# Turning the exponentials of the packed queries: from TensorE to VectorE and DMAs, with the value products a half step later

## The chip, the cores and the metric

The kernel runs on one core of a Trainium2 chip. The metric is the time of one execution on the device in microseconds (us). Its engines are TensorE (PE in the profile, with PEld for its weight loads), VectorE (DVE), ScalarE (ACT), GpSimd (POOL) and SyncE (SP), which here only issues DMAs.

## The reference

Two attentions after each other, then a Fourier mix over the sequence and the model dimension, a normalization and a feed-forward network. Batch 8, 8 heads, 576 tokens, 64 dimensions a head (model dimension 512), 32 packed queries a head, all in float32:

```python
p_packed = sm_attn(p, k, v)            # 32 packed queries look at 576 keys and values
out = sm_attn(q, p_packed, p_packed)   # 576 queries look at the 32 packed rows
# sm_attn(q, k, v): softmax(q @ k.T / sqrt(64)) @ v
x = out, heads side by side            # (8, 576, 512)
u = x + real(fft(fft(x, axis=1), axis=2))
un = (u - mean(u)) / sqrt(var(u) + 1e-6)
result = u + relu(un @ w_ch1) @ w_ch2  # 512 -> 2048 -> 512
```

## The kernel before

**Tiles.** The 8 x 576 rows of `u` go through the feed-forward network in nine tiles of 512 rows. In a tile (`ffn`) 16 pairs of products follow each other: `up(j)` (12 matmuls of 512 columns into the buffer `ph`, L857) and `down(j-1)` (12 matmuls into `acc`, L874). After `up(j)` ScalarE makes `hh` from `ph` and VectorE `hl` (L863, L864); `down(j)` uses both, one pair later. `ph` has one buffer only, so the next matmuls into it wait until `hl` has been made.

**Fronts.** The attention and the Fourier mix of batch b (`front(b)`, a generator) are made piece by piece between these products: `front(0)` ahead of all tiles, and `front(t + 1)` in tile t, up to batch 7. After `up(j)` comes half step 2j, after `down(j-1)` half step 2j+1. Half steps 0 and 2 finish the batch before; from half step 1 on each takes the next piece of the string `ORDER[min(b, 2)]`, in which `y` ends a piece. A piece in an even half step so stands between an up and a down product, one in an odd half step between a down and an up product.

**The pieces that matter.** Heads are worked on in two groups of four (g = 0, 1); 4 heads x 32 packed queries fill 128 partitions.

- `S` (`scores`): scores of the packed queries with the keys, their maxima, and on ScalarE the exponentials `e1` (128 x 576, L349).
- `X` (`turned_scores`): TensorE turns `e1` by matmuls with the identity, four 128 x 128 blocks and one of 64 columns for each group (L360, L363); ScalarE and VectorE copy them to `e1T` (L366, L367); VectorE takes the reciprocals of the sums.
- `p0 p1` (`packed`): the value products, for each group 5 chunks of tokens x 4 heads, `po += e1T.T @ vt` (L383). Four chunks have 128 rows and the last one 64. Each float32 matmul runs as two passes.
- `d0 d1`, `g0 g1`: the packed values turned, and their spectra (`pg`).
- `U` (`queries`): scores of the 576 queries with the packed values. The 512-wide parts and one narrow tail go to the shared banks, the other tail takes the buffer of `ph`:

```python
tails = [bank("s2Tt")] + ([psf.tile([P, 512], F32, tag="ph", name="s2Tt")] if len(gs) == 2 else [])
```

- `e0 e1`, `m0 a0 m1 a1`: second softmax, mostly on VectorE (L444, L445, L457 to L461, L498, L500).

**Order.** For TensorE, VectorE, ScalarE and GpSimd the order written is the order run (`manual_schedule`). SP's DMAs are put in order by the scheduler, those under `keep_in_program_order` as written. All loads go through SP's one queue. Keys, values and queries of a batch share two buffers (`ld`): the value loads `vt` (640 KB each) wait until `S` has read the keys, the query loads `qt` until `p0` and `p1` have read the values. A round trip through DRAM exists already: `send` writes a block of `u` (`far`, 256 KB) and reads it back in four parts (`back`).

Of the kernel before, what the change touches and what calls it, by code (L numbers as in the profile page):

```python
# [17 lines left out]
P = 128  # L18
S = 576
# [22 lines left out]
         "H1 v2 W10 P1",  # L42
         "K0 K1 Q0 Q1 y S V0 V1 y X y p0 p1 y d0 d1 y g0 y U y g1 y e0 y e1 y y m0 y a0 y m1 y a1 y f0 y r0 y h0 y f1 y r1 y "
         "h1 y y",
         "S y X y p0 p1 y d0 d1 y g0 y U y g1 y e0 y e1 y y m0 y a0 y m1 y a1 y f0 y r0 y h0 y f1 y r1 y "
         "h1 y y")


# [35 lines left out]
def tile_kernel(ctx, tc, kpT, qT, v, w1, w2, tabH, tabL, tabR, tabF, tabB, tabT, sel, ident_d, out):  # L84
# [182 lines left out]
    def load(src, shape, name, place=None, pinned=False):  # L267
        if isinstance(place, tuple):
            t = spot(*place, shape)
        elif place:  # L270
            t = work.tile(shape, F32, tag=place, name=name, bufs=2)
        else:
            t = ld.tile(shape, F32, tag="ld", name=name)
        sent = nc.sync.dma_start(t, src)
        if pinned:
            tc.keep_in_program_order(sent)
        return t
# [6 lines left out]
    def front(b):  # L284
# [16 lines left out]
            kps[g] = load(kpT[b, :, 2 * g:2 * g + 2, :], [P, 2, S + NPK], "kp")  # L301

        def load_values(g):
            vts[g] = load(v[b, :, g], [P, 5, 4 * D], "vt", (g, 4) if b == 0 else None, b == 1)

        def load_queries(g):
            qts[g] = load(qT[b, :, 2 * g:2 * g + 2, :], [P, 2, S], "qt", (g, 7) if b == 0 else (2, 0) if b == 1 and g == 0 else (2, 2 * S / DM) if b == 1 else None)
# [18 lines left out]
        def scores(*gs):  # L326
# [11 lines left out]
            for g in gs:  # L338
# [13 lines left out]
                in_place("x", g, exps)  # L352
                e1s[g], sums[g] = e1, sm2

        def turned_scores(*gs):
            tp = {}
            for g in gs:
                tp[g] = bank("e1tp")
                for c in range(4):
                    nc.tensor.transpose(tp[g][:, c * P:(c + 1) * P], e1s[g][:, c * P:(c + 1) * P], ident)  # L360
            tq = bank("e1tq")
            for g in gs:
                nc.tensor.transpose(tq[:D, g * P:(g + 1) * P], e1s[g][:, 4 * P:S], ident)  # L363
            for g in gs:
                e1T[g] = work.tile([P, 5, P], F32, tag="att", name="e1T", bufs=ATT)
                nc.scalar.copy(e1T[g][:, 0:4, :].rearrange("p c k -> p (c k)"), tp[g])  # L366
                nc.vector.tensor_copy(e1T[g][:D, 4, :], tq[:D, g * P:(g + 1) * P])  # L367
            for g in gs:
                ri, sm2 = small.tile([P, 1], F32, tag="ri", name="ri"), sums[g]
                nc.vector.tensor_scalar(ri, sm2[:, 0:1], sm2[:, 1:2], 1e-9, ALU.add, ALU.add)  # L370
                nc.vector.reciprocal(ri, ri)
                rinv[g] = ri

        def packed(g):

            if g not in vts:
                load_values(g)
            vt = vts[g]
            po = bank("po")
            for c in range(5):  # L380
                kk = P if c < 4 else D
                for h in range(4):
                    nc.tensor.matmul(  # L383
                        po[h * NPK:(h + 1) * NPK, :D], e1T[g][:kk, c, h * NPK:(h + 1) * NPK],
                        vt[:kk, c, h * D:(h + 1) * D], start=(c == 0), stop=(c == 4),
                        tile_position=(0, h * NPK))
            pp2 = work.tile([P, 2, D], F32, tag="pp2", name="pp2")
            nc.vector.tensor_scalar(pp2, po[:, :D].unsqueeze(1).to_broadcast([P, 2, D]), rinv[g], None, ALU.mult)
            pp2s[g] = pp2

            def spread():
                bd = work.tile([P, 4, D], F32, tag="tmp", name="bd", bufs=3)
                nc.gpsimd.tensor_tensor(bd, pp2[:, 0:1, :].to_broadcast([P, 4, D]),
                                        bmask.unsqueeze(2).to_broadcast([P, 4, D]), ALU.mult)

                def diagonals():
                    bdh[g] = work.tile([P, 4 * D], F32R, tag="bdh", name="bdh")
                    bdl[g] = work.tile([P, 4 * D], F32R, tag="bdl", name="bdl")
# [158 lines left out]
        def folded_parts(g):  # L557
# [10 lines left out]
            def low():  # L568
# [2 lines left out]

            in_place("H", g, low)

        parts = {"S": lambda _: scores(0, 1), "U": lambda _: queries(0, 1), "X": lambda _: turned_scores(0, 1),
                 "s": scores, "t": turned_scores, "p": packed, "d": packed_parts, "q": queries, "e": less_one, "m": less_mean, "g": values_spectrum, "a": weights, "f": folded, "r": folded_rest,
                 "h": folded_parts,
                 "T": load_tables, "B": lambda _: load_turn(), "K": load_keys, "V": load_values,
# [91 lines left out]
            ypx["p", 0] = value(xh, xl, slice(1, 256, 2))  # L669
            ypx["q", 0] = value(oh, ol, slice(1, 256, 2), psf.tile([P, 512], F32, tag="ph", name="px"))  # L670

        parts["P"], parts["X"] = first_products, lambda _: first_values() if b == 0 else turned_scores(0, 1)

        def idle(n, gate=None):
            w = gate if gate is not None else ubuf[:, NU - 1, 256:256 + P]
# [371 lines left out]
def _prepare(q, k, v, p, moe_w_ch1, moe_w_ch2):  # L1047
# [3 lines left out]
    def heads(x):  # L1051
        return x.transpose(0, 2, 1, 3).reshape(B, x.shape[2], DM)[:, :, col]

    def pairs(x):
# [3 lines left out]

    vv = np.zeros((B, 5 * P, DM), v.dtype)
    vv[:, :S] = heads(v)  # L1060
    arrays = {
        "kpT": np.concatenate([pairs(k), pairs(p)], 3), "qT": pairs(q[:, :, np.array(TOK), :]),
        "v": vv.reshape(B, 5, P, 2, 4 * D).transpose(0, 2, 3, 1, 4),
        "w1": moe_w_ch1[col].reshape(4, P, NJ, P).transpose(1, 2, 0, 3).reshape(P, NJ, DM),
        "w2": moe_w_ch2[:, col].reshape(NJ, P, DM).transpose(1, 0, 2),
    }
# [39 lines left out]
```

## Time and profile before

| | us |
|---|---|
| median of 3 runs (lowest to highest) | 983.49 (982.37 to 985.61) |
| profiled execution, its time | 983.41 |
| profiled execution, its span | 981.6 |
| TensorE busy (share of the span) | 958.2 (98%) |
| VectorE, ScalarE, GpSimd busy | 574.6, 458.0, 462.0 |

A busy time counts a matmul from its start to its modelled end, and matmuls overlap: 512-column matmuls show some 0.39 us each, but start 0.23 us apart. What a piece costs TensorE is therefore read from start to start in the timeline. A tile lasts about 105.5 us: the outputs of the first, second and third tile are issued from 165.61, 271.00 and 376.56 us on. The names in a row are `written<-read`, and a bracket at its end is the idle time ahead of it with what ended it.

### The profile page before, as it was taken

What the parts mean: (1) busy time and instruction counts of PE and PEld (TensorE: products, weight loads), DVE (VectorE), ACT (ScalarE), POOL (GpSimd) and SP (SyncE); (2) the same over time, 40 slices, a digit from 0 to 9 for tenths busy, and PEclk for the clock granted to TensorE, in tenths of its full rate; (3) what the DMA queues carried; (4) which work ended last, traced back from release to release, by engine and by line L of the source; (5) the groups of instructions that cost most, each with busy time, mean ns of one, the idle gap of its engine ahead of it and who ended that gap; (6) DMA issues with size and microseconds to landing.
All of it is one profiled execution on the core that took longest, in us unless ns stands there. A gap on an engine that the chain in (4) does not pass through costs nothing.

```text
span 981.6 us, 15190 instructions
## 1 busy us (share of the span) xinstructions
PE 958.2 (98%) x5682; PEld 782.5 (80%) x5682; DVE 574.6 (59%) x1184; ACT 458.0 (47%) x942; POOL 462.0 (47%) x397
## 2 busy tenths in 40 slices
PE   7899999999999999999999999999999999999998
PEld 4777787788877887788778887878777888887886
DVE  5988966487547855594658665784559451413111
ACT  5677655444444445444534545444443443334331
POOL 3146534454445534653455444543455354444542
PEclk9999999999999999999999999999999999999999
DMA  9565211300141012210330013110301010101001
GB/s 353 213 224 200 89 44 48 137 22 13 44 146 52 22 44 97 100 44 1 133 108 18 26 59 130 52 65 22 110 37 43 23 65 1 57 29 44 1 1 43
DMA packets 36968, 72.60 MB, mean 74 GB/s; under 512 B 4240, under 2 KB 18448, under 8 KB 36896
## 3 DMA queue, kind: packets, MB, share of 16 engines
q1 hardware_dynamic: 35856, 70.34, 20.7%
q0 software_dynamic: 1040, 1.31, 0.4%
q8 instruction: 44, 0.72, 0.3%
q14 instruction: 28, 0.23, 0.1%
HBM read 55.38 MB, written 16.25 MB: 73 GB/s over the span
## 4 chain that ended last, share of the span: by engine, by line
PE 83%; DVE 12%; ACT 2%; DMA 1%; issue 1%; POOL 0%; ACTq 0%; DVEq 0%; SPq 0%
PE ph L857 35%; PE acc L874 34%; DVE hl L864 1%; DVE s L498 1%; PE po L383 1%; DVE w2f L203 1%; PE px L282 1%; PE px L280 1%; PE px L281 1%; DMA wst<-w 1%; PE s L322 1%; PE e1tp L360 1%; PE py L280 1%; PE py L282 1%; PE py L281 1%
## 5 line engine op out<-in xcount | busy, mean ns | idle before, releaser
L110 POOL TENSOR_TENSOR wr_l<-w2f,wr_h 128x512 fp32r<-128x512 f32 x144 | 188.6, 1310 | 300.4 <-ACT wr_h L107 300.2
L110 POOL TENSOR_TENSOR wr_l<-w1f,wr_h 128x512 fp32r<-128x512 f32 x144 | 200.4, 1392 | 188.5 <-ACT wr_h L107 173.2
L864 DVE SCALAR_TENSOR_TENSOR hl<-ph,hh 128x512 fp32r<-128x512 f32 x144 | 98.7, 686 | 307.7 <-ACT hh L863 307.3
L857 PE MATMUL ph<-uh,wr_h 128*128 128x512 f32 (+1 forms) x580 | 228.7, 396 | 6.7 <-DVE hl L864 4.1
L874 PE MATMUL acc<-wr_h,hh 128*128 128x512 f32 x576 | 226.1, 392 | 0.0
L857 PE MATMUL ph<-ul,wr_h 128*128 128x512 f32 (+1 forms) x580 | 224.9, 389 | 0.5 <-DVE ul L110 0.5
L874 PE MATMUL acc<-wr_h,hl 128*128 128x512 f32 x576 | 224.9, 390 | 0.0
L874 PE MATMUL acc<-wr_l,hh 128*128 128x512 f32 x576 | 224.7, 390 | 0.0
L857 PE MATMUL ph<-uh,wr_l 128*128 128x512 f32 (+1 forms) x580 | 224.6, 389 | 0.0
L863 ACT ACTIVATE hh<-ph 128x512 fp32r<-128x512 f32 x144 | 86.2, 598 | 246.2 <-PE ph L857 232.5
L107 ACT CAST wr_h<-w1f 128x512 fp32r<-128x512 f32 x144 | 89.3, 620 | 175.1 <-PE acc L874 89.9
L857 PEld LDWEIGHTS ph<-uh,wr_h 128*128 128x128 f32 x580 | 108.5, 188 | 43.0 <-DVE hl L864 7.8
L857 PEld LDWEIGHTS ph<-uh,wr_l 128*128 128x128 f32 x580 | 108.5, 188 | 23.2
L874 PEld LDWEIGHTS acc<-wr_h,hl 128*128 128x128 f32 x576 | 108.1, 188 | 23.2
L857 PEld LDWEIGHTS ph<-ul,wr_h 128*128 128x128 f32 x580 | 108.6, 188 | 21.4 <-DVE ul L110 1.0
L874 PEld LDWEIGHTS acc<-wr_h,hh 128*128 128x128 f32 x576 | 108.1, 188 | 21.7
L874 PEld LDWEIGHTS acc<-wr_l,hh 128*128 128x128 f32 x576 | 108.2, 188 | 21.0
L107 ACT CAST wr_h<-w2f 128x512 fp32r<-128x512 f32 x144 | 88.6, 615 | 34.1 <-PE acc L874 26.9
L254 ACT ACTIVATE junk<-ubuf,stat 128x512 f32<-128x512 f32 x36 | 25.8, 718 | 3.3 <-DVE stat L249 3.3
L920 DVE SCALAR_TENSOR_TENSOR ubuf<-acc,stat,ubuf 128x512 f32<-128x512 f32 x36 | 24.5, 742 | 2.2 <-PE acc L874 2.2
L498 DVE TENSOR_TENSOR s<-s,z 128x576 f32<-128x576 f32 x16 | 24.7, 1541 | 0.5
L110 DVE TENSOR_TENSOR yl<-py,yh 128x258 fp32r<-128x258 f32 x32 | 13.2, 425 | 19.5 <-ACT yh L107 18.8
(229 smaller groups left out, 1229.5 us busy)
## 6 DMA issues: line engine op xcount, KB each, us to landing
kp<-kpT SPq DMA_DIRECT2D x16, 608.0 KB, 4.9
out<-ubuf SPq DMA_DIRECT2D x36, 256.0 KB, 2.1
vt<-v SPq DMA_DIRECT2D x14, 640.0 KB, 5.1
qt<-qT SPq DMA_DIRECT2D x12, 576.0 KB, 4.8
far<-unt SPq DMA_DIRECT2D x26, 256.0 KB, 2.0
back<-far SPq DMA_DIRECT2D x104, 64.0 KB, 2.0
w1f<-w SPq DMA_DIRECT2D x9, 512.0 KB, 7.2
w2f<-w SPq DMA_DIRECT2D x9, 512.0 KB, 6.6
```

What stands on the lines that cost most here:

```text
L107: copied = nc.scalar.copy(hi, src)
L110: (lo_eng or nc.vector).tensor_tensor(lo, src, hi.bitcast(F32), ALU.subtract)
L254: nc.scalar.activation(junk, u, AF.Square, bias=st[:, 1:2], scale=-sign, accum_out=st[:, 2:3])
L280: nc.tensor.matmul(o, lh, rh, start=first, stop=False)
L281: nc.tensor.matmul(o, lh, rl, start=False, stop=False)
L282: nc.tensor.matmul(o, ll, rh, start=False, stop=last)
L498: engw[g].tensor_tensor(s2s[g], s2s[g], broadcast(zs[g]), ALU.mult)
L857: nc.tensor.matmul(ph[:, t], l[:, c * P:(c + 1) * P], r[:, c, t], start=(k == 0), stop=(k == 11))
L863: nc.scalar.activation(hh[:, :T], ph[:, :T], AF.Relu)
L864: nc.vector.scalar_tensor_tensor(hl[:, :T], ph[:, :T], 0.0, hh[:, :T].bitcast(F32), ALU.max, ALU.subtract)
L874: nc.tensor.matmul(acc[i], l[:, w], r, start=(j == 0 and k == 0), stop=(j == NJ - 1 and k == 2))
L920: nc.vector.scalar_tensor_tensor(u, acc[i], stat_of[key][:, 2:3], u, ALU.mult, ALU.add)
```

## The change

For batches 2 to 7 the exponentials are no longer turned by TensorE. VectorE transposes `e1` in blocks of 32 x 32 (`e1b`), SP writes the result to DRAM (`fare`, 288 KB a group) and reads it back in four parts a group, so that `e1T` has tokens on its partitions, head by head (`scores_away`, piece `D`). `D` stands in the first piece, directly behind `S`; the order of SP's queue is fixed as first value load, the two writes, the eight reads, second value load. `X` keeps only the reciprocals. The value products come in half step 5 instead of 4, and everything up to `e1` a half step later; one empty half step ahead of `m0` is dropped, so `m0` and what follows keep their places.

The last two chunks of the value products have 96 rows in these batches. In batches 0 and 1, which keep the matmuls, the last chunk has 128 rows, with 64 tokens that the fourth chunk holds already set against zeros in the values, and the last turning matmul takes 128 columns. The host lays the values out to match.

```diff
-         "S y X y p0 p1 y d0 d1 y g0 y U y g1 y e0 y e1 y y m0 y a0 y m1 y a1 y f0 y r0 y h0 y f1 y r1 y "
+         "S V0 D V1 y X y y p0 p1 y d0 d1 y g0 y U y g1 y e0 y e1 y m0 y a0 y m1 y a1 y f0 y r0 y h0 y f1 y r1 y "
...
-            vts[g] = load(v[b, :, g], [P, 5, 4 * D], "vt", (g, 4) if b == 0 else None, b == 1)
+            vts[g] = load(v[b, :, g], [P, 5, 4 * D], "vt", (g, 4) if b == 0 else None, b > 0)
...
+        def chunk_rows(c):
+            return P if c < 3 or b < 2 else P - 32
+
+        def scores_away(*gs):
+            blocks = {}
+            for g in gs:
+                blocks[g] = work.tile([P, S], F32, tag="att", name="e1b", bufs=ATT)
+                nc.vector.transpose(blocks[g], e1s[g])
+            fars = {}
+            for g in gs:
+                fars[g] = dr.tile([P, S], F32, tag="fare", name="fare")
+                tc.keep_in_program_order(nc.sync.dma_start(fars[g], blocks[g]))
+            for g in gs:
+                e1T[g] = work.tile([P, 4, 5, NPK], F32, tag="att", name="e1T", bufs=ATT)
+                wide = e1T[g].rearrange("k h c p -> k h (c p)")
+                for r in range(4):
+                    n = NPK * (5 if r < 3 else 3)
+                    at = 5 * NPK * r
+                    back = nc.sync.dma_start(wide[r * 32:(r + 1) * 32, :, 0:n],
+                                             fars[g][:, at:at + n].rearrange("(h k) n -> k h n", h=4))
+                    tc.keep_in_program_order(back)
...
-                nc.tensor.transpose(tq[:D, g * P:(g + 1) * P], e1s[g][:, 4 * P:S], ident)
+                nc.tensor.transpose(tq[:, g * P:(g + 1) * P], e1s[g][:, S - P:S], ident)
...
-                kk = P if c < 4 else D
+                kk = chunk_rows(c)
...
-        parts["P"], parts["X"] = first_products, lambda _: first_values() if b == 0 else turned_scores(0, 1)
+        parts["P"], parts["X"] = first_products, lambda _: first_values() if b == 0 else turned_scores(0, 1) if b == 1 else score_sums(0, 1)
```

How the instructions stand. First TensorE at `U` of batch 3, in the third tile; before, it stands between a down product (L874) and an up product (L857):

```order
L874 MATMUL acc_3075<-wr_l,hh 128x512
L874 MATMUL acc_3075<-wr_h,hl 128x512
L322 MATMUL s2Tt<-qt,ppT 32x64 [waits DMAHW0_49,DVE_49]
L322 MATMUL s2Tt<-qt,ppT 32x64 [waits DMAHW1_49,DVE_49]
L322 MATMUL s2Tt<-qt,ppT 32x64 x6
L322 MATMUL s2T<-qt,ppT 32x512 [waits DVE_49] x2
L322 MATMUL s2T<-qt,ppT 32x512 x6
L857 MATMUL ph<-uh,wr_h 128x512 [waits DVE_49]
L857 MATMUL ph<-ul,wr_h 128x512
```

The same place after the change, where L885 is the up product and L902 the down product:

```order
L885 MATMUL ph<-ul,wr_h 128x512
L885 MATMUL ph<-uh,wr_l 128x512
L322 MATMUL s2Tt<-qt,ppT 32x64 [waits DMAHW4_49,DVE_49]
L322 MATMUL s2Tt<-qt,ppT 32x64 [waits DMAHW5_49,DVE_49]
L322 MATMUL s2Tt<-qt,ppT 32x64 x6
L322 MATMUL s2T<-qt,ppT 32x512 [waits PE_49] x2
L322 MATMUL s2T<-qt,ppT 32x512 x6
L902 MATMUL acc_3071<-wr_h,hh 128x512
L902 MATMUL acc_3071<-wr_l,hh 128x512 [waits Pool_49]
```

`U` has changed sides: it follows an up product now. Of its first two rows the second writes the tail that lies in the buffer of `ph`, so its wait on VectorE is one for the reader of the `ph` last written.

Next SP's queue, in the second tile; before, the two value loads, then the two query loads, then the keys of the next batch:

```order
L274 DMA vt<-v 128x1280 [waits PE_49]
L274 DMA vt<-v 128x1280 [waits DMAHW6_49,PE_49]
L274 DMA qt<-qT 128x1152 [waits DMAHW7_49,DMAHW5_49,PE_49]
L274 DMA qt<-qT 128x1152 [waits DMAHW6_49,DMAHW0_49,PE_49]
L274 DMA kp<-kpT 128x1216 [waits DMAHW7_49,DMAHW1_49,PE_49]
L274 DMA kp<-kpT 128x1216 [waits DMAHW2_49,DMAHW0_49,PE_49]
```

The same stretch after the change (DMAHW0 to 7 are the semaphores that landings raise):

```order
L274 DMA vt<-v 128x1280 [waits PE_49]
L368 DMA fare<-e1b 128x576 [waits DMAHW6_49,DVE_49]
L368 DMA fare<-e1b 128x576 [waits DMAHW7_49,DVE_49]
L375 DMA e1T<-fare 32x4x160 [waits DMAHW0_49,DMAHW6_49,Activation_49,Pool_49]
L375 DMA e1T<-fare 32x4x160 [waits DMAHW1_49]
L375 DMA e1T<-fare 32x4x160 [waits DMAHW2_49]
L375 DMA e1T<-fare 32x4x96 [waits DMAHW3_49]
L375 DMA e1T<-fare 32x4x160 [waits DMAHW4_49,DMAHW7_49,Activation_49,Pool_49]
L375 DMA e1T<-fare 32x4x160 [waits DMAHW5_49]
L375 DMA e1T<-fare 32x4x160
L375 DMA e1T<-fare 32x4x96
L274 DMA vt<-v 128x1280 [waits DMAHW0_49,PE_49]
```

The second value load has moved behind ten DMAs, of which the first reads wait for the writes to land and the writes for VectorE. The query loads follow it as before.

Last VectorE at the same time, before: behind the maxima of the scores it makes the `hl` of the second up product.

```order
L343 TENSOR_SCALAR nb<-mx_1997 128x1 [waits DVE_49]
L341 TENSOR_REDUCE mx_2006<-acc_1942 128x1
L341 TENSOR_REDUCE mx_2006<-s_1980 128x1 [waits PE_49]
L343 TENSOR_SCALAR nb<-mx_2006 128x1 [waits DVE_49]
L864 SCALAR_TENSOR_TENSOR hl<-ph,hh 128x512 [waits Activation_49]
L761 TENSOR_TENSOR xa<-px,spec_1971 64x512 [waits PE_49]
```

And after the change, where L892 makes `hl`:

```order
L343 TENSOR_SCALAR nb<-mx_1997 128x1 [waits DVE_49]
L341 TENSOR_REDUCE mx_2006<-acc_1942 128x1
L341 TENSOR_REDUCE mx_2006<-s_1980 128x1 [waits PE_49]
L343 TENSOR_SCALAR nb<-mx_2006 128x1 [waits DVE_49]
L364 STREAM_TRANSPOSE e1b<-e_2002 128x576 [waits Activation_49]
L364 STREAM_TRANSPOSE e1b<-e_2011 128x576 [waits Activation_49]
L892 SCALAR_TENSOR_TENSOR hl<-ph,hh 128x512 [waits Activation_49]
L789 TENSOR_TENSOR xa<-px,spec_1971 64x512 [waits PE_49]
```

Two transposes, each of which waits for ScalarE's exponentials, now stand ahead of that `hl`.

More of the change, by code (lines that the diff above doesn't have):

```diff
@@ L362, in turned_scores, with score_sums @@
             for g in gs:
-                nc.tensor.transpose(tq[:D, g * P:(g + 1) * P], e1s[g][:, 4 * P:S], ident)
+                nc.tensor.transpose(tq[:, g * P:(g + 1) * P], e1s[g][:, S - P:S], ident)
             for g in gs:
-                e1T[g] = work.tile([P, 5, P], F32, tag="att", name="e1T", bufs=ATT)
-                nc.scalar.copy(e1T[g][:, 0:4, :].rearrange("p c k -> p (c k)"), tp[g])
-                nc.vector.tensor_copy(e1T[g][:D, 4, :], tq[:D, g * P:(g + 1) * P])
+                t = work.tile([P, 5, P], F32, tag="att", name="e1T", bufs=ATT)
+                nc.scalar.copy(t[:, 0:4, :].rearrange("p c k -> p (c k)"), tp[g])
+                nc.vector.tensor_copy(t[:, 4, :], tq[:, g * P:(g + 1) * P])
+                e1T[g] = t.rearrange("k c (h p) -> k h c p", h=4)
+            score_sums(*gs)
+        def score_sums(*gs):
             for g in gs:
@@ L380, in packed @@
             for c in range(5):
-                kk = P if c < 4 else D
+                kk = chunk_rows(c)
                 for h in range(4):
                     nc.tensor.matmul(
-                        po[h * NPK:(h + 1) * NPK, :D], e1T[g][:kk, c, h * NPK:(h + 1) * NPK],
+                        po[h * NPK:(h + 1) * NPK, :D], e1T[g][:kk, h, c, :],
                         vt[:kk, c, h * D:(h + 1) * D], start=(c == 0), stop=(c == 4),
@@ L572, in folded_parts @@
             in_place("H", g, low)
-        parts = {"S": lambda _: scores(0, 1), "U": lambda _: queries(0, 1), "X": lambda _: turned_scores(0, 1),
+        parts = {"S": lambda _: scores(0, 1), "U": lambda _: queries(0, 1), "D": lambda _: scores_away(0, 1),
                  "s": scores, "t": turned_scores, "p": packed, "d": packed_parts, "q": queries, "e": less_one, "m": less_mean, "g": values_spectrum, "a": weights, "f": folded, "r": folded_rest,
@@ L1060, in _prepare @@
     vv[:, :S] = heads(v)
+    first = np.concatenate([vv[:2, :4 * P], vv[:2, -D:], vv[:2, 4 * P:S]], 1)
+    first = first.reshape(2, 5, P, 2, 4 * D).transpose(0, 2, 3, 1, 4)
+    later = vv[2:].reshape(B - 2, 4, 5, 32, 2, 4 * D).transpose(0, 1, 3, 4, 2, 5).reshape(B - 2, P, 2, 5, 4 * D)
     arrays = {
         "kpT": np.concatenate([pairs(k), pairs(p)], 3), "qT": pairs(q[:, :, np.array(TOK), :]),
-        "v": vv.reshape(B, 5, P, 2, 4 * D).transpose(0, 2, 3, 1, 4),
+        "v": np.concatenate([first, later]),
         "w1": moe_w_ch1[col].reshape(4, P, NJ, P).transpose(1, 2, 0, 3).reshape(P, NJ, DM),
```

## The prediction

> **What bounds the kernel now.** I read the page first (engine shares, chain), then the list of what TensorE waits for, and then the timeline of one tile, the third (270 to 376 us).
>
> ```profile
> span 981.6 us, 15190 instructions
> PE 958.2 (98%) x5682; PEld 782.5 (80%) x5682; DVE 574.6 (59%) x1184; ACT 458.0 (47%) x942; POOL 462.0 (47%) x397
> PE 83%; DVE 12%; ACT 2%; DMA 1%; issue 1%; POOL 0%; ACTq 0%; DVEq 0%; SPq 0%
> PE ph L857 <- DVE hl L864: 4.1, 3, 1.5
> ```
>
> TensorE is busy for 98% of the span and carries 83% of the chain; its largest wait, for `hl`, is 4.1 us in all. So inside a tile a microsecond taken from TensorE's row of work is a microsecond of the result, and so is one of new waiting; what the other engines do counts only where TensorE comes to wait for it. The profiled execution took 983.41 us, 1.8 around its span, and stands beside the median of 983.49; my sum is made against 983.41.
>
> **Removed: the turning matmuls (X).** In six tiles, those that prepare batches 2 to 7:
>
> ```profile
> 281.69 0.39 PE L874 MATMUL acc<-wr_h,hl 128*128 128x512 f32 x1
> 281.92 1.03 PE L360 MATMUL e1tp<-ident,e 128*128 128x128 f32 x8
> 282.79 0.38 PE L363 MATMUL e1tq<-ident,e 128*64 128x128 f32 x2
> 282.93 0.48 PE L857 MATMUL ph<-uh,wr_h 128*128 128x512 f32 x1
> 283.24 0.40 PE L857 MATMUL ph<-ul,wr_h 128*128 128x512 f32 x1
> 283.48 0.40 PE L857 MATMUL ph<-uh,wr_l 128*128 128x512 f32 x1
> ...
> 285.87 1.73 PE L383 MATMUL po<-vt,e1T 128*32 128x64 f32 x80
> 287.53 0.50 PE L874 MATMUL acc<-wr_h,hh 128*128 128x512 f32 x1
> ```
>
> A 512-wide matmul follows the one before by 0.23 (281.69 to 281.92). With X gone the up product starts at 281.92 instead of 282.93, 1.01 us earlier, and its first step is 0.23 instead of 0.31 (the step out of the 64-column form): **1.10 us a tile**. The copies of the turned rows on ScalarE and VectorE go too; TensorE waits for neither here, so they count as nothing.
>
> **One tile size in the value products.** Windows cut narrowly into L383 show the passes of four:
>
> ```profile
> 285.87 0.65 PE L383 MATMUL po<-vt,e1T 128*32 128x64 f32 x32
> 286.29 0.42 PE L383 MATMUL po<-vt,e1T 128*32 128x64 f32 x7
> 286.46 0.26 PE L383 MATMUL po<-vt,e1T 64*32 64x64 f32 x4
> 286.54 0.42 PE L383 MATMUL po<-vt,e1T 64*32 64x64 f32 x7
> 286.70 0.26 PE L383 MATMUL po<-vt,e1T 128*32 128x64 f32 x4
> ...
> 273.31 0.40 PE L857 MATMUL ph<-uh,wr_l 128*128 128x512 f32 x1
> 273.54 0.41 PE L602 MATMUL pz<-yr,tbr 101*128 101x258 f32 x2
> ```
>
> Eight passes of 128 rows start between 285.87 and 286.29, 0.06 apart. The step into the 64-row form is 0.17 (286.29 to 286.46), the one after it 0.08, the step back 0.16 (286.54 to 286.70): some 0.13 too much for each of three changes inside the two products, **0.40 us a tile**. The last chunks now hold 96 rows. L602, with 101 rows, follows a 128-row matmul after the usual 0.23, so a count between 64 and 128 costs no change; I take 96 like 101.
>
> The two batches that keep the matmul way gain too: the one prepared in the first tile 0.40 and the 0.08 of the 64-column step, 0.5 us; the first batch, where TensorE waits for other engines around these matmuls, between nothing and two changes (0.26), taken as 0.1. Together 0.6 us.
>
> **Moved: everything from the value products to `e` by a half step.** This is where I see the price. The score products U write one of their tails into the only buffer of `ph`, which the up product also uses. Before, U stands behind a down product, and the `ph` that it needs was read out during that product. Now U stands directly behind an up product, and has to wait until that product's `hh` and `hl` have been made.
>
> ```profile
> 296.39 0.39 PE L874 MATMUL acc<-wr_h,hl 128*128 128x512 f32 x1
> 296.70 0.34 PE L322 MATMUL s2Tt<-qt,ppT 64*32 64x64 f32 x16
> ...
> 300.46 0.40 PE L857 MATMUL ph<-uh,wr_l 128*128 128x512 f32 x1
> 300.95 0.60 ACT L863 ACTIVATE hh<-ph 128x512 fp32r<-128x512 f32 x1 [3.22 <-PE ph L857]
> 301.58 0.69 DVE L864 SCALAR_TENSOR_TENSOR hl<-ph,hh 128x512 fp32r<-128x512 f32 x1 [2.23 <-ACT hh L863]
> ```
>
> U starts 0.31 after the matmul before it. Here the last matmul of the up product starts at 300.46, so U could start at 300.77; `hl` ends at 302.27, and with a hop of 0.03 (as from `hh` to `hl`) the second matmul of U starts at 302.30. TensorE executes in order, so the whole queue behind it (the rest of U, the next down product) waits: **1.53 us a tile lost**. This wait hangs only on rows that the change doesn't touch, so its bounds are narrow: 1.4 and 1.7. Nothing covers it, and no stall of TensorE goes away in exchange (U had none).
>
> **Added: transposes on VectorE, two writes and eight reads on SP's queue, the second value load behind them.** All of this has to be done before the value products, which stand a half step later.
>
> ```profile
> 277.65 0.20 ACT L349 ACTIVATION_READ_ACCUMULATOR e<-s,nb 128x1 f32 x1
> 278.60 0.21 ACT L349 ACTIVATION_READ_ACCUMULATOR e<-s,nb 128x1 f32 x1
> 279.33 0.69 DVE L864 SCALAR_TENSOR_TENSOR hl<-ph,hh 128x512 fp32r<-128x512 f32 x1 [1.68 <-ACT hh L863]
> 317.71 0.78 DVE L500 STREAM_TRANSPOSE a<-s 128x576 f32<-128x576 f32 x1
> ...
> 219.47 0.33 SPq L786 DMA_DIRECT2D far<-unt  x1
> 221.53 1.75 SPq L791 DMA_DIRECT2D back<-far  x4
> 257.79 3.71 SPq L791 DMA_DIRECT2D back<-far  x8
> 275.73 1.39 SPq L274 DMA_DIRECT2D vt<-v  x2
> back<-far SPq DMA_DIRECT2D x104, 64.0 KB, 2.0
> DMA to landing us min/median/max: 3.9/3.9/3.9
> DMA to landing us min/median/max: 4.7/4.7/4.7
> ```
>
> The transposes (0.78 each, the size of L500) start when the exponentials end, 277.85 and 278.81, and end at 278.65 and 279.6; they fill VectorE's 1.68 of idleness and push `hl` from 279.33 to about 279.6. Its `ph` is wanted at 281.92, so that is free. The first write is issued at 278.70. From the issue of `far` (256 KB) to the first read behind it pass 2.06; a load of 640 KB takes 3.9 to land, so 32 KB more are worth some 0.15, and a write of 288 KB 2.2. So the reads start at 280.9, eight take 3.71 as for `back`, and the second value load is issued at 284.6; before, it stood right behind the first one of 275.73. The two landing rows are those of this tile's first value load (3.9) and first query load (4.7, 576 KB), each ahead of its partner in the queue: 288.5 to 289.3, and I take 288.6, since the 3.9 is for the same 640 KB. TensorE, without X, would start the first value products at 287.5 (one up and one down product after 281.92) and the second, ten passes of 0.06 later, at 288.1. So it waits **0.5 us a tile** for values; the turned exponentials themselves (last read issued by 284.5, landing 2.0 later as `back` does) are in time. Behind the value load in SP's queue stand the query loads; they need the buffers of the value products anyway, so they are issued at 288.1 and some 289, land by 294 even with the 4.7, and U comes at about 300. Ends: nothing, if the reads issue or the load lands 0.5 faster, and 1.3, with the 4.7.
>
> The Trainium skill, page "VectorE: DVE Perf Modes", section "The three transpose paths", speaks against such a path: it sends a 128x128 transpose to TensorE where PSUM will do, and calls a plain DMA copy with a strided pattern 19 times slower than the hardware's DMA transpose. The round trip of this kernel, with 512-byte runs, doesn't show that price, and the new reads have runs of 640 and 384 bytes.
>
> **Later in the tile.** `e0` and `e1` now both stand between two `hl`.
>
> ```profile
> 620.66 1.57 DVE L445 TENSOR_TENSOR s<-s,m 128x576 f32<-128x576 f32 x1
> 623.80 0.74 DVE L444 TENSOR_REDUCE m<-s 128x18 f32<-128x576 f32 x1
> 624.58 1.08 DVE L445 TENSOR_TENSOR s<-s,m 128x576 f32<-128x576 f32 x1
> 628.57 0.69 DVE L864 SCALAR_TENSOR_TENSOR hl<-ph,hh 128x512 fp32r<-128x512 f32 x1 [2.91 <-ACT hh L863]
> ```
>
> They take 0.74+1.57+0.74+1.08, with gaps 4.2 us, in the 4.8 from 623.80 to 628.57: room of 0.6, or none if both subtractions take 1.57. I count nothing, and up to 0.3 us a tile at the other end.
>
> **Sum.** A tile: -1.10 -0.40 +1.53 +0.50 = +0.53; six tiles +3.2; the two other batches -0.6: +2.6, so 983.41 becomes 986.0, 0.26% more, just inside what a measurement of this kernel can tell from no change (about 0.3%, from 980.5 to 986.4).
>
> **Rivals.** (1) The values come in time, the 0.5 is nothing: 983.0. For it: 0.5 is the end of a chain of ten steps, each good to 0.1. (2) Slower: the second value load decides. If it lands like the query load, or the ten DMAs issue more slowly, TensorE waits 1.3 a tile: 6 x 0.8 more, 990.8. It makes the kernel measurably slower from 0.6 us a tile on. For it: of the two rows one shows 4.7. Against: the row of its own size shows 3.9. (3) Faster: U doesn't wait, since `ph` is free after all, and only the values cost: 986.0 - 9.2 = 976.8. Against it: the order shows U's second matmul behind the up product with a wait on VectorE, whose count in the built program is the one that this up product's `hl` raises. (4) 96 rows count as a tile size of their own: 2.4 more, 988.4. Against: the 101-row matmuls. (5) VectorE falls behind at `e1`: up to 1.8 more, 987.8. (6) The turning path is slow as such, a read taking 19 times the 2 us of `back`: e1T would come near 319, some 31 us late in each tile, +190 us. The skill's sentence above would say so; the rows of `back` say the opposite, and the runs here aren't single elements.
>
> **Chances.** Forecast (values 0.25 to 0.8 late; 984.5 to 987.8) 0.47; (1) 0.19; (2) 0.16; (3) 0.08; (4) 0.05; (5) 0.04; (6) 0.01. Faster by over 0.3%: (3), 0.08. Within: (1) and some 0.27 of the forecast, whose threshold lies at 0.57 us of waiting, 0.46. Slower: the rest, 0.46. The range from 982.0 (rival 1 with U's wait at 1.4) to 990.5 leaves out (3), (6) and the end of (2), about 0.15; the forecast's own range is 984.5 to 987.8.
>
> **What would show it.** In the profile after: L360 and L363 only in the first two batches, and up products that follow down products 0.23 later near 281.9; passes of the value products 0.06 apart without a long step; a TensorE wait of 1.5 us at U, put down to `hl`, in six tiles; one of about half a microsecond at the second value products, put down to the value load; `hl` before 280.4 in the third tile; no wait for `e1T`. I am wrong if U starts 0.31 behind the up product, if the second value load is issued before the reads, or if a new wait for VectorE shows late in the tiles.

## The result and the profile after

| | before | after |
|---|---|---|
| median of 6 runs each, us (lowest to highest) | 983.86 (982.37 to 985.61) | 989.73 (987.76 to 990.58) |
| ratio after to before, 95% interval | | 1.0061 [1.0049, 1.0074] |
| profiled execution, time / span | 983.41 / 981.6 | 989.80 / 988.0 |

The changed kernel is slower by 0.6%. The head of its page (span, busy times, chain) and the top of the list of what TensorE waits for (total, times, longest):

```profile
span 988.0 us, 15216 instructions
PE 951.6 (96%) x5622; PEld 776.0 (79%) x5622; DVE 581.3 (59%) x1184; ACT 452.2 (46%) x930; POOL 465.9 (47%) x397
PE 76%; DVE 12%; DMA 5%; ACT 3%; issue 1%; SPq 1%; POOL 0%; ACTq 0%; DVEq 0%
...
PE s2Tt L322 <- DVE hl L892: 7.5, 6, 1.2
PE po L411 <- DMA vt<-v: 5.0, 6, 1.4
```

TensorE has 60 matmuls and 6.6 us of work less, and the span is 6.4 longer. Two new waits, six times each, stand at the top: `U` for `hl`, and the value products for the value load. DMAs now carry 5% of the chain. No wait of the six tiles is put down to the reads of `e1T`. The third tile in the timeline (it starts at 273.44 instead of 270.81), first TensorE and VectorE:

```profile
280.51 0.78 DVE L364 STREAM_TRANSPOSE e1b<-e 128x576 f32<-128x576 f32 x1 [0.22 <-ACT e L349]
281.48 0.78 DVE L364 STREAM_TRANSPOSE e1b<-e 128x576 f32<-128x576 f32 x1 [0.19 <-ACT e L349]
282.18 0.65 DVE L892 SCALAR_TENSOR_TENSOR hl<-ph,hh 128x512 fp32r<-128x512 f32 x1
...
284.32 0.39 PE L902 MATMUL acc<-wr_h,hl 128*128 128x512 f32 x1
284.54 0.39 PE L885 MATMUL ph<-uh,wr_h 128*128 128x512 f32 x1
284.77 0.39 PE L885 MATMUL ph<-ul,wr_h 128*128 128x512 f32 x1
...
290.08 0.77 PE L411 MATMUL po<-vt,e1T 128*32 128x64 f32 x40
291.43 0.77 PE L411 MATMUL po<-vt,e1T 128*32 128x64 f32 x40 [0.59 <-DMA vt<-v]
...
301.31 0.30 PE L322 MATMUL s2Tt<-qt,ppT 64*32 64x64 f32 x2
302.11 0.69 DVE L892 SCALAR_TENSOR_TENSOR hl<-ph,hh 128x512 fp32r<-128x512 f32 x1 [1.11 <-ACT hh L891]
302.85 0.28 PE L322 MATMUL s2Tt<-qt,ppT 64*32 64x64 f32 x7 [1.25 <-DVE hl L892]
```

Where `X` stood, the up product (284.54) follows the down product at 0.22. The value products are two closed blocks of 40 passes without a long step inside, but apart: four heads run beside each other, so a block is ten steps of 0.06, the second could have started at 290.68 (290.08 and ten steps) and started at 291.43, 0.75 later. `U` begins at 301.31 and stands until `hl` has ended: 302.85, 1.54 later.

SP's queue in the same tile, and the landing of its first and of its second value load:

```profile
278.36 0.34 SPq L274 DMA_DIRECT2D vt<-v  x1
281.32 1.28 SPq L368 DMA_DIRECT2D fare<-e1b  x2
283.50 3.65 SPq L375 DMA_DIRECT2D e1T<-fare  x8
287.24 0.38 SPq L274 DMA_DIRECT2D vt<-v  x1
...
DMA to landing us min/median/max: 4.0/4.0/4.0
DMA to landing us min/median/max: 3.9/3.9/3.9
```

Counted from the first value load, the writes are issued at +2.96, the reads at +5.14, the second value load at +8.88; it lands at +12.8.

**The balance by tile.** From the first up product of a tile to the next one's, in us, tiles 1 to 8 (the fronts of batches 2 to 7 are made in tiles 2 to 7):

| tile | 1 | 2 | 3 | 4 | 5 | 6 | 7 | 8 |
|---|---|---|---|---|---|---|---|---|
| before | 115.40 | 105.55 | 105.56 | 105.07 | 105.07 | 106.94 | 106.84 | 88.79 |
| after | 115.52 | 106.84 | 106.32 | 106.87 | 106.15 | 106.82 | 107.57 | 88.79 |

The six tiles lose 5.5 us together. Ahead of the first tile another 1.2 are lost, and 0.5 come back behind the last.

### The profile page after: what moved, and what is told of

Same layout as the page of the kernel before. It is cut to its first block, busy times and chain, and to the rows that moved or that the text cites. A ratio compares the mean times of both kernels' runs of the same rounds, so it can differ in the third digit from the quotient of the medians.

```text
span 988.0 us, 15216 instructions
## 1 busy us (share of the span) xinstructions
PE 951.6 (96%) x5622; PEld 776.0 (79%) x5622; DVE 581.3 (59%) x1184; ACT 452.2 (46%) x930; POOL 465.9 (47%) x397
## 3 DMA queue, kind: packets, MB, share of 16 engines
q0 software_dynamic: 1040, 1.31, 0.4%
## 4 chain that ended last, share of the span: by engine, by line
PE 76%; DVE 12%; DMA 5%; ACT 3%; issue 1%; SPq 1%; POOL 0%; ACTq 0%; DVEq 0%
PE ph L885 33%; PE acc L902 32%; DMA vt<-v 2%; DVE hl L892 2%; DVE s L526 1%; SPq L375 1%; DMA w1f<-w 1%; DVE w2f L203 1%; PE px L282 1%; PE px L280 1%; PE px L281 1%; DMA wst<-w 1%; ACT hh L891 1%; DMA fare<-e1b 1%; PE py L280 1%
## 5 line engine op out<-in xcount | busy, mean ns | idle before, releaser
L110 POOL TENSOR_TENSOR wr_l<-w1f,wr_h 128x512 fp32r<-128x512 f32 x144 | 202.9, 1409 | 178.6 <-ACT wr_h L107 163.8
L892 DVE SCALAR_TENSOR_TENSOR hl<-ph,hh 128x512 fp32r<-128x512 f32 x144 | 98.6, 685 | 294.1 <-ACT hh L891 293.8
L885 PE MATMUL ph<-uh,wr_h 128*128 128x512 f32 (+1 forms) x580 | 228.0, 395 | 5.6 <-DVE hl L892 2.9
L902 PE MATMUL acc<-wr_h,hh 128*128 128x512 f32 x576 | 226.5, 393 | 0.0
L885 PE MATMUL ph<-ul,wr_h 128*128 128x512 f32 (+1 forms) x580 | 224.8, 389 | 0.5 <-DVE ul L110 0.5
L902 PE MATMUL acc<-wr_h,hl 128*128 128x512 f32 x576 | 224.9, 390 | 0.0
L902 PE MATMUL acc<-wr_l,hh 128*128 128x512 f32 x576 | 224.7, 390 | 0.0
L885 PE MATMUL ph<-uh,wr_l 128*128 128x512 f32 (+1 forms) x580 | 224.5, 389 | 0.0
L885 PEld LDWEIGHTS ph<-uh,wr_h 128*128 128x128 f32 x580 | 108.5, 188 | 38.2 <-DVE hl L892 7.8
L902 PEld LDWEIGHTS acc<-wr_h,hh 128*128 128x128 f32 x576 | 108.2, 188 | 26.5 <-issue 5.0
L885 PEld LDWEIGHTS ph<-uh,wr_l 128*128 128x128 f32 x580 | 108.5, 188 | 23.0
L902 PEld LDWEIGHTS acc<-wr_h,hl 128*128 128x128 f32 x576 | 108.2, 188 | 23.1
L885 PEld LDWEIGHTS ph<-ul,wr_h 128*128 128x128 f32 x580 | 108.6, 188 | 21.3 <-DVE ul L110 1.0
L902 PEld LDWEIGHTS acc<-wr_l,hh 128*128 128x128 f32 x576 | 108.2, 188 | 21.1
L508 DVE TENSOR_TENSOR turned<-pg,turn 128x516 f32<-128x516 f32 x32 | 20.7, 688 | 12.6 <-PE pg L503 12.2
```

What stands on the lines that cost most here:

```text
L110: (lo_eng or nc.vector).tensor_tensor(lo, src, hi.bitcast(F32), ALU.subtract)
L508: nc.vector.tensor_tensor(x, pg[:, :N2].unsqueeze(1).to_broadcast([P, 2, N2]), w, ALU.mult)
L885: nc.tensor.matmul(ph[:, t], l[:, c * P:(c + 1) * P], r[:, c, t], start=(k == 0), stop=(k == 11))
L892: nc.vector.scalar_tensor_tensor(hl[:, :T], ph[:, :T], 0.0, hh[:, :T].bitcast(F32), ALU.max, ALU.subtract)
L902: nc.tensor.matmul(acc[i], l[:, w], r, start=(j == 0 and k == 0), stop=(j == NJ - 1 and k == 2))
```

## The experiments

All were timed in five rounds against the kernel before on the same chip; its medians there were 983.66 (30 runs) for the first four, 983.5 (11) for the next four, 982.53 (11) for the last. A "gap" is from one matmul's start to the next one's.

**1. Query scores behind a down product.** `U` and `g0` change places, so that `U` stands where its buffer is free:

```diff
-  "S V0 D V1 y X y y p0 p1 y d0 d1 y g0 y U y g1 y ..."
+  "S V0 D V1 y X y y p0 p1 y d0 d1 y U y g0 y g1 y ..."
```

> The changed kernel with one swap: U in half step 7 (behind a down product) and g0 in half step 8; nothing else differs. Theory (U's second tail waits for the buffer of ph, 1.46 us in each of six tiles in the changed kernel's trace): the TensorE wait of U for hl is gone, U starts 0.3 us behind the down product, and the time falls by 6 x 1.46 = 8.8 us, from 989.7 to 981, which is 0.997 of the time before; the wait for the second value load stays at about 1 us a tile. Rival (the lost time is given back as a wait elsewhere, VectorE being late from the moved half step on): the wait at U goes, but waits of TensorE for VectorE grow later in the tiles and the time stays above 986, ratio over 1.002.

Measured: 982.01 us (979.12 to 985.22), ratio 0.9982 [0.9969, 0.9996]. Its waits of TensorE:

```profile
PE po L411 <- DMA vt<-v: 5.1, 6, 1.2
...
PE ph L885 <- DVE hl L892: 4.1, 3, 1.5
```

The wait of `U` is gone from the list, the wait for the values stands as it was. From its first matmul to the product behind it `U` takes 1.26 us on the mean of the six tiles instead of 2.67, together 8.5 less, and the six tiles are 7.7 shorter. 1.2 are paid elsewhere: the gap ahead of an up product late in the sixth tile, 0.75 in the changed kernel, is 1.91 again, as it was before (last section).

**2. Both value loads first.** `V1` ahead of `D`, all else as in the changed kernel:

```diff
-  "S V0 D V1 y X ..."
+  "S V0 V1 D y X ..."
```

> The changed kernel with the second value load moved ahead of the two writes and eight reads in SP's queue (V0 V1 D); nothing else differs. Theory (the second value load is issued 8.9 us behind the first and its landing ends TensorE's wait at the second value products, 5.9 us over six tiles): it is issued 0.4 us behind the first, the wait for vt goes, and the reads of e1T land by some 0.4 us before the products need them; the time falls by 5 to 6 us to about 984, ratio 1.000 to 1.002. The wait at U stays at 1.46 a tile. Rival (the reads then come late, since the writes queue behind 640 KB more on the DMA engines): TensorE waits for e1T in place of vt, by 0.5 us or more at each of the value products, and the time stays at 987 to 990.

Measured: 986.54 us (985.09 to 989.59), ratio 1.0036 [1.0023, 1.0048]. A wait of TensorE, the third tile in SP's queue, and the writes in the list of DMAs (KB each, median us from issue to landing):

```profile
PE po L411 <- DMA e1T<-fare: 2.3, 3, 1.2
...
275.97 1.61 SPq L274 DMA_DIRECT2D vt<-v  x2
278.93 1.29 SPq L368 DMA_DIRECT2D fare<-e1b  x2
284.37 3.64 SPq L375 DMA_DIRECT2D e1T<-fare  x8
...
fare<-e1b SPq DMA_DIRECT2D x12, 288.0 KB, 3.9
```

The wait for the values is gone from the list, and half of it comes back as a wait for `e1T` (from start to start 3.1 us in the six tiles, where 6.0 were lost to the values). The writes land 3.9 us after issue on the median instead of 2.1; in the third tile it is 5.4, and the reads start at +8.4 there instead of +5.1. So both were half right: in two tiles nothing waits, as the theory had it, and in four the products wait 0.3 to 1.4 us, two of them over the 0.5 of the rival.

**3. Both edits together.**

```diff
-  "S V0 D V1 y X y y p0 p1 y d0 d1 y g0 y U y g1 y ..."
+  "S V0 V1 D y X y y p0 p1 y d0 d1 y U y g0 y g1 y ..."
```

> Both moves at once: the second value load ahead of the writes and reads, and U in half step 7 with g0 behind it. Theory (the two waits are all that eats the gain): no wait of TensorE over 0.2 us in the six tiles up to e1; the gain of 1.1 us (turning matmuls) and 0.4 us (tile size) a tile is seen whole, 6 x 1.5 and 0.6 in the other batches: 974 to 976, ratio 0.990 to 0.993 of the time before. Rival (the gain is lost to VectorE late in the tiles, where e0 and e1 now follow each other directly): waits of TensorE for hl late in the tiles grow, and the time stays at 979 or more, ratio over 0.995.

Measured: 979.72 us (975.61 to 984.24), ratio 0.9957 [0.9939, 0.9974]: less gain than the theory had, and the time of the rival, but not by its mechanism. TensorE's wait for `hl` late in the tiles is 4.1 us, no more than the 4.1 of the kernel before. What is left at the value products is the wait of experiment 2:

```profile
PE po L411 <- DMA e1T<-fare: 3.2, 4, 1.0
```

Against the changed kernel the six tiles gain 8.9 us, where the two waits were worth 15. From start to start the value products still wait 3.8, `U` takes 1.8 more than before the change (in two tiles it also waits for a query load, 0.5 each), and the sixth tile's gap is 1.91 again.

**4. One tile size alone.** The kernel before, with 128 rows in all chunks of the value products, in all batches, and 128 columns in the last turning matmul; matmuls still turn the exponentials, and the host lays the values out to match:

```diff
-                nc.tensor.transpose(tq[:D, g * P:(g + 1) * P], e1s[g][:, 4 * P:S], ident)
+                nc.tensor.transpose(tq[:, g * P:(g + 1) * P], e1s[g][:, S - P:S], ident)
...
-                kk = P if c < 4 else D
+                kk = P
```

> The kernel before with one part of the change alone: every batch keeps the turning matmuls, the order and the loads of before, but the last turning matmul takes 128 columns and all five chunks of the value products have 128 rows, with zeros in the values against tokens that are there twice. Theory (a change of the tile size costs TensorE some 0.13 us, three in the value products and one behind the turning matmuls): 0.40 + 0.08 us less in each of seven tiles, 0.1 to 0.3 in the first batch, so 3.5 us faster, ratio 0.9960 to 0.9970, and the passes of the value products 0.06 us apart throughout. Rival (the long steps are the price of a new group of weights or a new bank, not of the size): the steps stay and the time doesn't change, ratio 0.999 to 1.001.

Measured: 981.6 us (979.91 to 984.43), ratio 0.9978 [0.9969, 0.9987]. In the timeline of the third tile the value products are one block without steps:

```profile
288.85 1.32 PE L411 MATMUL po<-vt,e1T 128*32 128x64 f32 x80
290.11 0.50 PE L902 MATMUL acc<-wr_h,hh 128*128 128x512 f32 x1
```

From 288.85 to 290.11 are 1.26, where they took 1.66 before. The six tiles lost 2.36 us together, 0.39 each: the 0.40 of the prediction for the three steps in the value products. The further 0.08 that the expectation had for the 64-column step doesn't show: behind the last turning matmul, which now has 128 columns, the up product's first step is still 0.31 (285.91 to 286.22). So that long step doesn't come from the 64-column form. The time fell by 2.1 us where 3.5 were expected. The profiled execution itself can't be compared as a whole, because a lower clock was granted in its first tile (0.89 from 50 to 66 us and 0.93 from 84 to 110, where the profile before has 1.00 in both).

**5. The half step taken back.** The turning path of the changed kernel, but the value products in half step 4 as before, `U` behind a down product again, and (since the values are wanted sooner) both value loads first:

```diff
-  "S V0 D V1 y X y y p0 p1 y d0 d1 y g0 y U y g1 y e0 y e1 y m0 ..."
+  "S V0 V1 D y X y p0 p1 y d0 d1 y g0 y U y g1 y e0 y e1 y y m0 ..."
```

> The changed kernel with the value products back in half step 4, where they were before the change, the query scores so back behind a down product, and both value loads ahead of the writes and reads. Theory (the half step later is what the nine microseconds of the path through memory need): no wait of the query scores for VectorE and none for the second value load, together -2.5 us a tile against the changed kernel, but the last reads land some 12 us after the first value load was issued and the value products now stand some 3 us earlier, at about +9, so the value products wait 2 to 4 us a tile for e1T: 985 to 999 us, 1.001 to 1.015 of before. Rival (the path is short enough, the half step was not needed): no wait anywhere, about 975, ratio 0.991.

Measured: 999.68 us (995.65 to 1008.41), ratio 1.0176 [1.0139, 1.0212]. Its largest wait of TensorE, and the writes in the list of DMAs:

```profile
PE po L411 <- DMA e1T<-fare: 21.4, 12, 3.4
...
fare<-e1b SPq DMA_DIRECT2D x12, 288.0 KB, 4.9
```

The value products of both groups wait in all six tiles, 3.6 us a tile in the list and 3.8 from start to start, at the upper end of the 2 to 4 that were expected, since here the writes took 4.9 us to land. The time is just above the expected range. The profiled execution, the slowest of the six at 1008.41, shows one more cost that the expectation lacked: behind these stalls a lower clock was granted. In the fourth tile it is 0.50 from 404 to 406 us and 0.69 from 406 to 408, and the first matmuls of the down product there start 0.42 to 0.60 apart instead of 0.23. An estimate from the lengths of the six tiles: 635.0 us before, less 9.0 won, and 22.8 of stalls are 648.8; they took 658.8, so some 10 us went to slower matmuls and whatever else came with the stalls. The path through memory needs the half step; the price of `U` is what the half step costs in the place where `U` then stands. Why the writes land later here than in experiment 2, in the same order of SP's queue, no run tells.

**6. The other tail in a shared bank.** The changed kernel in its order; only the buffer differs:

```diff
-            tails = [bank("s2Tt")] + ([psf.tile([P, 512], F32, tag="ph", name="s2Tt")] if len(gs) == 2 else [])
+            tails = [bank("s2Tt")] + ([bank("s2Tt") if b > 1 else psf.tile([P, 512], F32, tag="ph", name="s2Tt")] if len(gs) == 2 else [])
```

> The changed kernel, with its order, but the second narrow tail of the query scores in a shared bank instead of the buffer of ph (batches 2 to 7). Theory (the wait of the query scores is the wait for that one buffer and for nothing else): the gap of 1.46 us ahead of the second tail's first matmul is gone in all six tiles, at most some 0.3 us for a shared bank comes in its place; the second value load stays late by 1.0 us a tile; 981 to 984 us, ratio 0.998 to 1.000, as with the query scores moved. Rival (any place behind an up product costs this wait, because VectorE is what the shared banks wait for too): 988 to 990 us, ratio 1.005.

Measured: 989.72 us (988.70 to 991.93), ratio 1.0065 [1.0053, 1.0078]. The rival was right and my theory wrong. A wait of TensorE, and the timeline of the third tile:

```profile
PE s2T L322 <- DVE s L466: 3.3, 6, 0.5
...
300.43 1.02 PE L322 MATMUL s2T<-qt,ppT 64*32 64x512 f32 x2
301.09 0.69 DVE L892 SCALAR_TENSOR_TENSOR hl<-ph,hh 128x512 fp32r<-128x512 f32 x1 [1.13 <-ACT hh L891]
301.70 0.37 DVE L466 STREAM_TRANSPOSE s<-s2Tt 128x64 f32<-128x64 f32 x2
301.99 0.18 PEld L322 LDWEIGHTS s2T<-qt,ppT 64*32 64x32 f32 x14 [1.45 <-DVE s L466]
303.01 0.50 PE L902 MATMUL acc<-wr_h,hh 128*128 128x512 f32 x1
```

`U` writes four buffers, and there are three shared ones (`ps`, `bufs=3`) and that of `ph`. Without `ph`, the last 512-wide part needs the bank of the first tail, which VectorE empties (L466) behind the same `hl`. The gap inside `U` is 1.13 in all six tiles instead of 1.46, but this saves nothing: from its first matmul to the down product `U` takes 2.71 us (300.30 to 303.01), in the changed kernel 2.67, before 1.13. So the wait belongs to the place behind an up product: with the buffer of `ph` `U` waits for `hl`, without it for a bank that VectorE empties only behind that `hl`, and not to the one buffer that the prediction named.

**7. The second value load between the reads.** Experiment 1, and SP's order is first value load, two writes, four reads of group 0, second value load, four reads of group 1:

```diff
-  "S V0 D V1 y X ..."
+  "S V0 D y X ..."
...
+                if g == gs[0]:
+                    load_values(1)
```

> The kernel with the query scores ahead of the spectrum of group 0 (behind a down product), and the second value load in the middle of SP's queue: first value load, two writes, four reads of group 0, second value load, four reads of group 1. Theory (SP's issue time and the landing time of 4 us decide): the second value load is issued at +7.0 us instead of +8.9, lands at +11 ahead of its use at +12.3, and the reads of group 1, at +7.4 to +8.9 plus 2.1, land by +11 too; neither wait is left: 974 to 977 us, ratio 0.991 to 0.993. Rival (transfers behind a load of 640 KB land late whatever they are): the reads of group 1 land 3.5 to 5 us after issue, at +12 to +14, and the products of group 1 wait 0.5 to 1.2 us in half of the tiles or more: 978 to 982 us, ratio 0.994 to 0.998.

Measured: 978.79 us (976.57 to 980.55), ratio 0.9951 [0.9936, 0.9967]; the rival's time, and by its mechanism. No wait for values is left, but one for the reads behind the load, which land 3.5 to 5.3 us after issue; from start to start the products lose 3.9 us in the six tiles (the list of TensorE's waits, then that of DMAs):

```profile
PE po L413 <- DMA e1T<-fare: 2.5, 3, 1.4
...
e1T<-fare SPq DMA_DIRECT2D x36, 80.0 KB, 3.0
```

**8. The second value load cut in two.** Experiment 1, with chunks 0 and 1 (256 KB) ahead of the writes, and 2 to 4 (384 KB) behind the reads. `G1` and `L1` issue the two parts:

```diff
-  "S V0 D V1 y X ..."
+  "S V0 G1 D L1 y X ..."
```

> The kernel with the query scores ahead of the spectrum of group 0, and the second value load cut in two: chunks 0 and 1 (256 KB) ahead of the writes, chunks 2 to 4 (384 KB) behind the reads. Theory (late is what is issued last, by some 1 us): the last 384 KB are issued at the same +9 us, land about 1 us sooner than 640 KB did and are wanted some 0.9 us later, at chunk 2; the writes behind 640 + 256 KB land 0.3 to 1 us later, which the room of the reads holds; no wait left or some 0.2 us a tile: 975 to 978 us, ratio 0.991 to 0.994. Rival (the writes are pushed as they were behind both loads): the value products of group 0 wait for e1T about 1 us in half of the tiles: 979 to 982 us, ratio 0.995 to 0.998.

Measured: 976.50 us (974.98 to 977.87), ratio 0.9928 [0.9916, 0.9940], the theory's time. Its wait is larger than expected, some 0.5 us a tile from start to start instead of at most 0.2. The wait, and the DMAs concerned:

```profile
PE po L418 <- DMA vt<-v: 2.4, 4, 1.1
...
fare<-e1b SPq DMA_DIRECT2D x12, 288.0 KB, 2.7
vt<-v SPq DMA_DIRECT2D x6, 384.0 KB, 3.4
```

The writes land 0.6 us later than in the changed kernel and still in time; the last 384 KB land after 3.4 us, and are wanted only at the third chunk. Half of the wait for values is left. This version beats both kernels, but not by the cut alone: in both places of the last section, in the sixth and the seventh tile, it has the short gap (0.77 and 0.75), where experiment 1 has 1.91 twice. That is 2.3 us.

**9. Both: the cut, and the later part between the reads.**

```diff
-  "S V0 G1 D L1 y X ..."
+  "S V0 G1 D y X ..."
...
+                if g == gs[0]:
+                    load_last_chunks(1)
```

> Both at once: the second value load cut in two (chunks 0 and 1 ahead of the writes, chunks 2 to 4 later), and its later part, 384 KB, between the reads of group 0 and those of group 1; the query scores ahead of the spectrum of group 0. Theory (what stands behind a large load in the queue lands later by some 1 us for each 640 KB ahead of it, and everything has to have landed by +11.7 to +12.3): the 384 KB are issued some 1.8 us sooner than with the cut alone and are in time in all tiles; the reads of group 1 land 2.1 to 3 us after issue, by +12 at the latest, and cost at most some 0.3 us in two or three tiles: 973.5 to 976 us, ratio 0.990 to 0.992. Rival (the bytes ahead of them decide, not the place in the queue: the same 2.4 MB are then always late for something): the wait only moves from the values to the reads of group 1, 0.5 to 1 us in half of the tiles: 976 to 978 us, ratio 0.992 to 0.995.

Measured: 978.11 us (976.37 to 979.90), ratio 0.9953 [0.9940, 0.9966]: the rival, just above its range. The wait moves from the values to the reads of group 1, which land 2.8 to 4.0 us after issue behind the 384 KB, those of group 0 ahead of it about 2.0. In the list of TensorE's waits:

```profile
PE po L420 <- DMA e1T<-fare: 1.8, 3, 0.8
```

From start to start the products lose 2.9 us in the six tiles, 3.1 in experiment 8. In the profiles 9 is the slower one by 0.8 us in these tiles, and has the long gap of 1.92 in the seventh, where 8 has 0.75. So whether this order is itself worse than that of experiment 8 is not shown.

## Why the prediction was nearly right, and which term was too small

The time, 989.73, lies in the range and above the forecast's own (984.5 to 987.8), between the forecast (986.0) and rival 2 (990.8). The forecast of 0.26% left open whether a difference could be measured; the 0.61% is clear.

| term, us a tile | predicted | measured |
|---|---|---|
| X removed | -1.10 | -1.10 (0.22 and 0.23 where 1.24 and 0.31 stood) |
| one tile size | -0.40 | -0.39 (experiment 4) |
| `U` waits for `hl` | +1.53 | +1.54 (301.31 to 302.85) |
| second value load late | +0.50 | +1.00 (0.75 in the third tile) |
| sum of a tile | +0.53 | +1.05 |

Six times 1.05 are 6.3, and 1.2 less of waiting for VectorE in the sixth tile leave 5.1, against 5.5 measured.

- **X and the tile size** came as worked out, and 96 rows cost no change of size (rival 4 falls: no long step in the blocks of 290.08 and 291.43, 0.77 each). One reading was wrong: the prediction put the first step of the up product, 0.31 instead of 0.23, down to the 64-column form. Experiment 4 still has 0.31 with 128 columns. The step goes with `X`, so the 1.10 stands; the 0.08 more that was counted for the second batch does not.
- **`U`** cost what was predicted, and experiment 1 shows the place as its cause. The mechanism was told too narrowly: experiment 6 shows that another buffer doesn't help.
- **The second value load is the term that was mis-sized.** Its stalls in the six tiles are 1.25, 0.75, 1.59, 0.93, 0.89 and 0.59. The chain of ten steps that led to it held in the third tile to 0.1 (issue at +8.88 where 8.87 was predicted, use at +12.32 for 12.37). It was wrong in what it took to be equal in all tiles or left out: the load is issued at +9.09 on the mean of the six (8.84 to 9.33: in the second tile the writes took 2.5 to land instead of 2.1, in the fifth they were issued 0.28 later, in the fourth the eight reads took 4.02 of the queue instead of 3.65, in the sixth 0.41 pass behind the last read), it takes 4.08 to land (3.9 to 4.5) where 4.0 was taken, and from the landing to the matmul pass another 0.14, which I had not counted. 0.22 + 0.08 + 0.14 + 0.05 (used sooner) are the missing 0.5. All four go the same way, and the slack of such a chain is small: each is under a quarter of a microsecond. Rival 2 gave a price of 1.3 to a load that lands like the query load, or to ten DMAs that issue more slowly; the first was so in one tile (4.5), the second in that same tile, the fourth.
- **The two other batches** were to bring 0.6. The second batch's, in the first tile, doesn't show (115.40 and 115.52), and ahead of the first tile 1.2 us were lost. But that stage isn't steady from one profile to the next with the same first front. The first up product in the timelines of the kernel before, of the changed one and of experiment 6:

```profile
49.86 0.74 PE L857 MATMUL ph<-uh,wr_h 128*128 128x256 f32 x4 [0.68 <-ACT uh L107]
51.08 0.74 PE L885 MATMUL ph<-uh,wr_h 128*128 128x256 f32 x4 [0.68 <-ACT uh L107]
49.80 0.74 PE L885 MATMUL ph<-uh,wr_h 128*128 128x256 f32 x4 [0.67 <-ACT uh L107]
```

  So these 1.2 us are not put down to the change, and whether 0.6 were won there stays open. 1.8 of the 3.7 between 986.0 and the result lie here; 3.0 are the value load, and 1.2 of VectorE's wait go the other way. Both 1.2 us are chance, as far as the prediction goes: it foresaw neither. Without the gain the time would have been some 990.9, outside the range of 982.0 to 990.5; without the loss ahead of the first tile, 988.5. That it lies inside is in part luck.
- **VectorE** took the transposes free of charge: `hl` at 282.18 is 279.55 in the time of the kernel before, where 279.6 was predicted. There is no new wait at `e1` (rival 5 falls).
- **The turning path** isn't slow as such (rival 6 falls): its reads land in 2.1 us. The Trainium skill, page "VectorE: DVE Perf Modes", section "The three transpose paths", warns of a plain DMA copy whose strides do the transposing, with a large innermost stride at the destination, and its factor of 19 is against the hardware's DMA transpose. Here VectorE has turned the 32 x 32 blocks and the DMAs move runs of 384 to 640 bytes. So that warning is about another form of copy, which no run here shows. The advice to use TensorE for a 128x128 transpose, which the prediction names beside it, stands in the next section of that page, "Rules for kernel authors" of the Trainium skill.

So what the change was worth in TensorE's own row, 1.5 us a tile, is real: with the wait of `U` removed and half of the one for values (experiment 8) the kernel is 0.7% faster than before. Its six tiles gain 6.7 us: 9.0 won and 2.3 of VectorE's wait, less 3.1 of waiting for values and 1.0 in `U`, come to 7.2. In the order that it came in, the half step put `U` in a place that costs as much, and the ten DMAs put the second value load behind its use.

## What to carry to other kernels

When a step is moved by one place to give a long path time, look at every later step that moves along, and at which buffers it needs there: here the one that moved from behind a down product to behind an up product cost all that was won. When the end of a chain of DMAs is forecast to be late by less than a microsecond, take it as late by that plus the spread of each link in all places, not in the one that was looked at. On one queue, changing the order moved the wait to the transfer that then stood behind the large one (experiments 2, 7, 9). Cutting the large one, with the part that is wanted first ahead, left the least waiting at the value products: 3.1 and 2.9 us in experiments 8 and 9, against 3.8, 3.9 and 6.0 in 3, 7 and 1. The difference to 3 and 7 is smaller than the 1.2 us by which VectorE's gaps move each of these times.

## What the runs showed of the hardware that was not expected

**A transfer behind a large one lands later.** The writes of 288 KB land 2.1 us after issue behind one value load of 640 KB that was issued 3 us ahead of them, 2.7 behind 640 and 256 KB, 3.6 to 4.9 behind two of 640 (medians of experiments 2, 3 and 5); reads of 48 to 80 KB take 2.1, 2.8 to 4.0 directly behind 384 KB and 3.5 to 5.3 behind 640.

**Hundredths of a microsecond between VectorE and GpSimd go with 1.2 us.** The long gap late in the sixth tile, in the timelines before (the up product waits for the `hl` of 653.38) and after, and the same place of the seventh tile after:

```profile
651.12 1.31 POOL L110 TENSOR_TENSOR wr_l<-w2f,wr_h 128x512 fp32r<-128x512 f32 x1 [1.51 <-ACT wr_h L107]
651.14 1.57 DVE L781 TENSOR_SCALAR unp<-ubuf,stat 128x512 f32<-128x512 f32 x1
654.08 0.50 PE L857 MATMUL ph<-uh,wr_h 128*128 128x512 f32 x1 [1.52 <-DVE hl L864]
...
658.37 0.48 DVE L809 TENSOR_SCALAR unp<-ubuf,stat 128x512 f32<-128x512 f32 x1
658.43 1.59 POOL L110 TENSOR_TENSOR wr_l<-w2f,wr_h 128x512 fp32r<-128x512 f32 x1 [1.58 <-ACT wr_h L107]
660.23 0.50 PE L885 MATMUL ph<-uh,wr_h 128*128 128x512 f32 x1 [0.36 <-DVE hl L892]
...
764.90 1.62 DVE L809 TENSOR_SCALAR unp<-ubuf,stat 128x512 f32<-128x512 f32 x1
764.93 1.31 POOL L110 TENSOR_TENSOR wr_l<-w2f,wr_h 128x512 fp32r<-128x512 f32 x1 [1.55 <-ACT wr_h L107]
```

Where GpSimd starts 0.02 us ahead, VectorE's subtraction takes 1.57 instead of 0.48, and the up product starts 1.91 behind the matmul before it; where VectorE starts 0.06 ahead, GpSimd's takes 1.59 instead of 1.31 and the gap is 0.75. In this place of the sixth and seventh tile, in all eleven kernels profiled here, a subtraction of 1.54 to 1.62 goes with a gap of 1.9 and one of 0.48 with 0.75 to 0.77. VectorE's is the short one in five of the 22 places, those in which it starts 0.04 to 0.06 ahead. The Trainium skill has a rule for this, page "SBUF — State Buffer", section "Who interferes with whom": the two share a pair of ports, and the order of issue decides which of them is blocked. The trace agrees in that one of the two always grows, and in 19 of the 22 places it is the one that starts second. In the other three (the rows of 764.90, and the seventh tile in experiments 6 and 9) VectorE starts first, by at most 0.03 us, and still is the one that grows; so the starts of the profile don't settle who wins. No experiment here moved one of the two on purpose, so the cause stays argued. But these 1.2 us belong in every comparison of two orders here: experiments 1 and 3 lose them again in the sixth tile, and experiment 8 wins them in both.
